# A decode kernel whose first transfer becomes sixteen runs of K's first chunk

## The chip, the cores and the metric

The kernel runs on one core of a Trainium2 chip. The metric is device time in microseconds (us), less is better. The time before is the median of three runs; one further execution was profiled.

## The reference

One decoding step: attention over a window of a cache, and beside it a small mixer with an MLP, both fed by the same normalized input. All tensors are bf16.

```python
xn = _layernorm(x, axis=-1)                                   # x: 4 x 1 x 576
return x + _A_ref(xn, A_k_cache, A_v_cache, A_wq, A_wo) + _B_ref(xn, B_w1, B_w2, B_w3, B_w4)

# A: 32 query heads, 16 key/value heads, Dh = 128, the last W = 2048 of 8192 positions
q = (x @ wq) per head;  k, v = the window of the caches
o = softmax(q k^T * Dh ** -0.5) v
A = o @ wo                                                    # wq: 576 x 4096, wo: 4096 x 576

# B: S = 1, so that the shifts leave the halves of h empty
h  = gelu(layernorm(x) @ w1);  x1 = x + shifted(h) @ w2       # w1, w2: 576 x 576
B  = x1 + gelu(layernorm(x1) @ w3) @ w4                       # w3: 576 x 4608, w4: 4608 x 576
```

## The kernel before

Nearly all of the data is read once: the K window and the V window (32 MB each), `wq`, `w3`, `w4` and `wo` of about 5 MB each, `w1` and `w2` of 0.65 MB each. All these transfers are issued on SyncE's queue (SP). Only the input `x` and the output go over ScalarE's queue.

Each engine has a program of its own. The list `prog[engine]` is sorted by a key that is written by hand, and the engine issues its list in that order. A transfer that has to wait for a buffer waits on SP, and all that stands behind it in SP's list waits with it. `add_dma(pairs, skey, waits, key)` (line 194) puts one transfer for each pair into the list; its issue is line 199. Each transfer adds 16 to the semaphore named by `skey` when it has landed. SP's order at the start is `w1` (key -50), `w2` (-49), `wq` (-48), `w3` (-47), then the chunks of K with keys 0, 1, 2 and so on. The first two chunks wait for nothing. Chunks 2 and 3 wait until the query is computed (`q`), since `wq` lies in their place. From chunk 4 on, each waits until TensorE has transposed the chunk four before it.

A chunk of K (`kv_src`) is one batch entry and four key/value heads: 128 runs of 64 positions, 16 KB each, 2 MB together. Its source is a view of 32 x 4 runs, and run (i, g) goes to partition 4 i + g of one of four slots of `kring` (`kslot`). There are 16 chunks, so a loop of four turns goes over the four slots. In the loop TensorE waits, ahead of a slot's first block, for the slot's semaphore:

```python
landed = e.snap(16 * it + 16)
...
if j % NBLK == 0:
    e.wait_ge(S["k", j // NBLK], landed)
```

For each chunk TensorE transposes eight blocks (line 485), VectorE and ScalarE copy them from PSUM (lines 469 and 468), and TensorE forms the scores (line 492). Ahead of the loop stands the small chain: two layernorms of `x` (lines 305 to 318), the mixer with `w1` (line 397) and `w2` (line 405), the query with `wq` (line 369), and the first half of the MLP with `w3` (line 430). The last entry of that program makes TensorE wait for a GpSimd constant. After the loop come the softmax (lines 498 to 535), eight chunks of V of 4 MB (line 553), and the products with `w4` and `wo` (line 392).

Of the kernel before, what the change touches and what calls it, by code (L numbers as in the profile page):

```python
# [37 lines left out]
def bass_parallel_sum__sliding_block_cached__mixer_s_mlp__decode_kernel(  # L38
# [31 lines left out]
    with ExitStack() as ctx:  # L70
        def sb(name, shape, dt):
            return ctx.enter_context(nc.sbuf_tensor(name, shape, dt))

        def sem(name):
            return ctx.enter_context(nc.semaphore(name))
# [5 lines left out]
        kslot = lambda s: kring[:, s * UE:(s + 1) * UE]  # L81
# [49 lines left out]
        perm_bf = sb("perm_bf", [128, 128], BF16)  # L131
# [39 lines left out]
        S = {}  # L171
# [16 lines left out]
        def add(engine, emit, waits=(), sig=None, key=0.0, inc=None):  # L188
            seqc[0] += 1
            prog[engine].append(Op(emit, waits, sig, key, seqc[0], inc))  # L190

        def add_dma(pairs, skey, waits=(), key=0.0, engine="sp"):
            if skey not in S:
                S[skey] = sem("s_" + "_".join(str(k) for k in (skey if isinstance(skey, tuple) else (skey,))))
            dma_count[skey] = dma_count.get(skey, 0) + 16 * len(pairs)

            def emit(e):
                for o_, i_ in pairs:
                    e.dma_start(o_, i_).then_inc(S[skey], 16)  # L199
            add(engine, emit, waits, None, key)  # L200
            return ("dma", skey, dma_count[skey])
# [48 lines left out]
        for gl in range(2):  # L250
            for x in range(2 * NVS):
# [3 lines left out]
                  waits=["pick11"], sig=f"pick2{gl}{x}", key=-84 + 0.1 * (8 * gl + x))  # L255


        def mask_of(t, tag, view):
            add("dve", lambda e: e.tensor_reduce(out=t[:], in_=view, axis=AX.X, op=ALU.add), waits=["ident_f"], sig=tag, key=-8)
        add("dve", lambda e: e.tensor_reduce(out=par[:], in_=ident_f[:].rearrange("p (m a) -> p a m", a=2), axis=AX.X, op=ALU.add),  # L260
            waits=["ident_f"], sig="par", key=-29.5)
# [13 lines left out]
        def kv_src(cache, c):  # L275
            b, gq = CH[c]
            return cache[b, NU * gq:NU * gq + NU, Sk - W:Sk, :].rearrange("g (i t) d -> i g (t d)", t=NT)
# [7 lines left out]
        t_done = lambda c: f"T{NBLK * c + NBLK - 1}"  # L285
        for c in range(NC):
            w = [t_done(c - N_CB)] if c >= N_CB else (["q"] if c >= 2 else [])
            add_dma([(kslot(c % N_CB), kv_src(A_k_cache, c))], ("k", c % N_CB), w, c)
        for c in range(NCV):
            w = [f"PV{2 * (c - NVS) + 1}"] if c >= NVS else [t_done(NC - N_CB + 2 * c - 3)] if c >= 2 else ["h2_1"]  # L290
# [93 lines left out]
        for k in range(2):  # L384
            for g in range(2):
# [3 lines left out]
                    waits=["qTp"] + (["qpad_zero"] if k + g == 0 else []), sig=f"qT{2 * k + g}", key=-10 + 0.1 * k)  # L389
# [18 lines left out]
        for h in range(2):  # L408
# [3 lines left out]
                waits=[f"hs{h}"], sig="x1" if h else "x1a", key=-27 + 0.1 * h)  # L412
# [3 lines left out]
            waits=["hT", "ln3_sd"], sig="gelu_h", key=-25.9)  # L416
# [38 lines left out]
        def pe_MO(t0, t1):  # L455
# [4 lines left out]
                        ins = acc_mm(e, h, h2T_sb[:, t, :], w4_t[:, t, HALF * h:HALF * (h + 1)])  # L460
                return ins
            return f
        add("pe", lambda e: e.wait_ge(S["pool"], resolve("perm_bf")[1]), waits=["qT3"], key=-1)


        def evac(n):
# [4 lines left out]
        for n in range(NB):  # L471
            c, k = n // NBLK, n % NBLK
            if k == 0:
                add("dve", lambda e, c=c: e.tensor_copy(out=Qs[:, c % N_CB, :], in_=Qpad_t[:, 128 * (4 * CH[c][0] + CH[c][1]):][:, 0:128]),
                    waits=[f"SC{c - 2}"] if c >= 1 else ["qT3"], key=n)
# [12 lines left out]
        def emit_SC(e, k):  # L488
# [11 lines left out]
            waits=["rmax"], sig="negb", key=KS + 0.05)  # L500
        for q in range(4):
            add("act", lambda e, q=q: e.activation(out=P_sb[:, q, :], in_=Sps[:, q, :], func=ACTF.Exp,
                                                   bias=negb[:, 0:1], scale=scale, accum_out=rs4[:, q:q + 1]),
                waits=["negb"], sig=f"exp{q}", key=KS + 0.1 + 0.01 * q)
# [16 lines left out]
        for qt in range(4):  # L521
            k0 = KS + 0.9 + 0.1 * qt
            add("pe2", pe_PT(qt), waits=[f"PTx{q}" for q in range(4)] + (["pick217"] + [f"E{NB - 1 - k}" for k in range(4)] if qt == 0 else []),
                sig=f"PTp{qt}", key=k0)
            if qt % 2 == 1:
                add("dve", lambda e, qt=qt: e.tensor_copy(out=PT_t[:, 512 * qt:512 * (qt + 1)], in_=ps[:, 4 + qt, :]),
                    waits=[f"PTp{qt}"], sig=f"PT{qt}", key=k0)
            else:
                add("act", lambda e, qt=qt: e.activation(out=PT_t[:, 512 * qt:512 * (qt + 1)], in_=ps[:, 4 + qt, :], func=ACTF.Copy),
                    waits=[f"PTp{qt}"], sig=f"PT{qt}", key=k0)  # L530
# [3 lines left out]
            waits=["rinv", "ident_f"], sig="diag", key=KS + 0.82)  # L534
        add("pe2", lambda e: e.matmul(rinvps, lhsT=ones_f[:], rhs=diag[:], start=True, stop=True),
            waits=["diag", "ones_f", "PT1"], sig="rinvp", key=KV + 0.5)
        add("dve", lambda e: e.tensor_copy(out=rinvB[:].rearrange("p (c u e) -> p c u e", u=NU, e=2),
                                           in_=rinvps.rearrange("p (u c e) -> p c u e", u=NU, e=2)),
            waits=["rinvp"], sig="rinvB", key=KV - 2)
# [29 lines left out]
        for bp in range(NPAIR):  # L569
            k0 = KV + 2 * NVS * (bp + 1) - 0.5  # L570
            add("dve", lambda e: e.tensor_scalar(out=tmp[:], in0=ps[:, 0, 128:256], scalar1=maskd[:, 1:2], scalar2=None, op0=ALU.mult),  # L571
                waits=[f"PV{2 * NVS * (bp + 1) - 1}", "maskd"], sig=f"F{bp}", key=k0)
# [4 lines left out]
                waits=["rinvB", f"fold{bp}"], sig=f"O{bp}", key=k0 + (3 if bp == 0 else 0.2))  # L577
# [5 lines left out]
            waits=["OR"], sig="ORT", key=KE + 0.3)  # L583
# [42 lines left out]
        def resolve(w):  # L626
            if isinstance(w, tuple):
                return S[w[1]], w[2]
            s_, val = ev_val[w]
            return S[s_], val  # L630
# [20 lines left out]
        e = nc.tensor  # L651
        emit_program("pe", "pe", e)
        with nc.Fori(0, N_LOOP, engines=[PE]) as it:
# [7 lines left out]
            for j in range(LB):  # L661
                emit_T(e, j, wait)
                if j % NBLK == 2:
                    k = (j // NBLK - 1) % N_CB
# [53 lines left out]
```

## Time and profile before

| what | value |
|---|---|
| median of three runs | 213.97 us (213.81 to 213.98) |
| the profiled execution, its own time | 213.93 us |
| its span, first to last instruction | 212.6 us |
| TensorE busy | 172.5 us, 81% of the span |
| VectorE, ScalarE, GpSimd busy | 111.9, 58.6, 15.6 us |
| DMA | 88.65 MB, mean 417 GB/s |

The profile's page gives, after the busy times of the engines, the span in 40 equal slices: a digit is the busy share of a slice in tenths, and the rows for DMA give the share of 16 DMA engines and the GB/s. A DMA row of a queue has packets, MB and the share of 16 engines' span that the packets took. In a table of windows each row has the stretch, the busy time and number of instructions of each engine, the TensorE clock, the share of the DMA engines and GB/s. Rows of a timeline begin with start and duration and may end with the idle time before and what ended it; "SPq" is SyncE issuing transfers. Lists of issues have the size of one transfer and the median time from issue to landing.

### The profile page before, as it was taken

Reading aid. Unit: us, or ns where it says so; the run is one execution under the profiler, and the core shown is the slowest. Engines: PE = TensorE matmul, PEld = TensorE weight load, DVE = VectorE, ACT = ScalarE, POOL = GpSimd, SP = SyncE. Lnnn points to the kernel's source line nnn. Section 1 sums busy time; section 2 is a strip of 40 time slices with the busy share of each in tenths; the row PEclk is TensorE's granted clock in tenths of the full one; section 3 lists DMA queues with packets and bytes.
Section 4 is the critical chain, followed back from the end, with each engine's and each line's share of the span. In section 5 each row is a group of like instructions: output and inputs, shape, how many; then the busy total and the mean of one; then the engine's idle time right before and its main releaser. Section 6 shows DMA issues by size and latency. Waiting matters only on the chain.

```text
span 212.6 us, 4856 instructions
## 1 busy us (share of the span) xinstructions
PE 172.5 (81%) x2212; PEld 133.7 (63%) x2216; DVE 111.9 (53%) x168; ACT 58.6 (28%) x69; POOL 15.6 (7%) x38
## 2 busy tenths in 40 slices
PE   1456147999999999999996089999989598997495
PEld 0222014888878888887774048988868487883262
DVE  5433200477776777777764869995575444003000
ACT  2004001366665566666656520000000000000000
POOL 8991000000000000000000000000000000000000
PEclk9997855899999999999999589999999889999799
DMA  6999999999999999999999999999999999999993
GB/s 242 453 444 445 429 396 416 432 425 427 429 416 438 432 422 429 435 422 424 432 444 438 444 407 459 413 425 453 407 444 438 419 425 410 451 476 393 407 408 131
DMA packets 5066, 88.65 MB, mean 417 GB/s; under 512 B 568, under 2 KB 704, under 8 KB 1216
## 3 DMA queue, kind: packets, MB, share of 16 engines
q1 hardware_dynamic: 5040, 88.49, 97.7%
q8 instruction: 8, 0.13, 0.3%
q14 instruction: 2, 0.02, 0.0%
q10 hardware_dynamic: 16, 0.01, 0.0%
HBM read 88.49 MB, written 0.00 MB: 416 GB/s over the span
## 4 chain that ended last, share of the span: by engine, by line
DMA 47%; PE 45%; DVE 4%; SPq 1%; ACT 1%; issue 1%
PE ps L485 23%; DMA vring<-in_A_wo_dram 15%; DMA vring<-in_B_w_dram 13%; DMA vring<-in_A_v_cache_dram 12%; PE ps L553 11%; DMA kring<-in_A_k_cache_dram 7%; PE ps L492 6%; PE ps L430 2%; SPq L199 1%; DVE vring L520 1%; DVE rmax L498 1%; DVE ktb L545 1%; PE ps L514 1%; PE ps L347 1%; ACT ktb L468 0%
## 5 line engine op out<-in xcount | busy, mean ns | idle before, releaser
L469 DVE COPY ktb<-ps 128x1024 bf16<-128x1024 bf16 x80 | 53.8, 689 | 23.5 <-PE ps L485 23.4
L485 PEld LDWEIGHTS ps<-perm_bf,kring 128*128 128x128 bf16 x1024 | 58.2, 98 | 8.3 <-issue 7.6
L485 PE MATMUL ps<-perm_bf,kring 128*128 128x128 bf16 x1024 | 61.7, 220 | 0.2
L468 ACT ACTIVATE ktb<-ps 128x1024 bf16<-128x1024 bf16 x48 | 48.0, 1023 | 32.5 <-PE ps L485 32.1
L545 DVE TENSOR_TENSOR ktb<-kring,mH_bf 128x4096 bf16<-128x4096 bf16 x16 | 36.2, 2286 | 14.6 <-PE ps L553 14.6
L553 PE MATMUL ps<-vring,ktb 128*128 128x256 bf16 x256 | 30.3, 282 | 4.3 <-DMA vring<-in_A_v_cache_dram 3.5
L553 PEld LDWEIGHTS ps<-vring,ktb 128*128 128x128 bf16 x256 | 25.7, 101 | 8.5 <-issue 3.6
L553 PE MATMUL ps<-kring,ktb 128*128 128x256 bf16 x256 | 28.6, 273 | 0.9 <-DMA kring<-in_A_v_cache_dram 0.9
L553 PEld LDWEIGHTS ps<-kring,ktb 128*128 128x128 bf16 x256 | 25.0, 98 | 4.5 <-issue 1.1
L608 ACT ACTIVATE out_sb<-ps 4x288 bf16<-4x288 f32 x1 | 0.4, 399 | 84.6 <-PE ps L392 84.6
L492 PE MATMUL ps<-ktb,Qs 128*32 128x512 bf16 x272 | 17.8, 382 | 1.2 <-ACT ktb L468 1.2
L430 PE MATMUL ps<-vring,xs 128*8 128x320 bf16 (+1 forms) x72 | 4.5, 429 | 7.6 <-DMA vring<-in_B_w_dram 7.6
L492 PEld LDWEIGHTS ps<-ktb,Qs 128*32 128x32 bf16 x272 | 5.7, 96 | 6.7 <-DVE ktb L469 1.4
L514 PE MATMUL ps<-vring,pick_bf 128*32 128x256 bf16 x64 | 3.9, 411 | 6.4 <-DVE rinv L532 6.4
L609 DVE CAST out_sb<-ps 4x288 bf16<-4x288 f32 x1 | 0.4, 449 | 15.7 <-PE ps L392 15.7
L392 PE MATMUL ps<-vring,h2T_sb 128*4 128x288 bf16 x72 | 6.2, 347 | 3.1 <-DMA vring<-in_B_w_dram 3.1
L571 DVE TENSOR_SCALAR tmp<-ps,maskd 128x128 f32<-128x128 f32 x2 | 0.7, 350 | 14.8 <-PE ps L553 14.8
L430 PEld LDWEIGHTS ps<-vring,xs 128*8 128x8 bf16 x72 | 2.1, 110 | 9.8 <-DMA vring<-in_B_w_dram 8.0
L330 PE MATMUL ps<-ident_bf,xp_bf 4*128 4x4 bf16 x15 | 0.8, 163 | 8.1 <-DVE xp_bf L314 5.0
L392 PEld LDWEIGHTS ps<-vring,h2T_sb 128*4 128x4 bf16 x72 | 3.7, 101 | 5.8 <-DMA vring<-in_B_w_dram 3.6
L514 PEld LDWEIGHTS ps<-vring,pick_bf 128*32 128x32 bf16 x64 | 2.0, 118 | 8.2 <-DVE rinv L532 6.9
L239 POOL MEMSET ktb<- 128x8192 bf16 x1 | 6.9, 6924 | 0.0
(93 smaller groups left out, 78.6 us busy)
## 6 DMA issues: line engine op xcount, KB each, us to landing
kring<-in_A_k_cache_dram SPq DMA_DIRECT2D x16, 2048.0 KB, 13.8
vring<-in_A_v_cache_dram SPq DMA_DIRECT2D x4, 4096.0 KB, 24.6
kring<-in_A_v_cache_dram SPq DMA_DIRECT2D x3, 4096.0 KB, 34.0
vring<-in_B_w_dram SPq DMA_DIRECT2D x2, 5184.0 KB, 25.1
kring<-in_A_wq_dram SPq DMA_DIRECT2D x1, 4608.0 KB, 15.7
kring<-in_A_v_cache_dram SPq DMA_DIRECT2D x2, 2048.0 KB, 27.4
vring<-in_A_wo_dram SPq DMA_DIRECT2D x1, 1872.0 KB, 26.9
vring<-in_A_wo_dram SPq DMA_DIRECT2D x1, 1440.0 KB, 29.8
```

Of the source, the lines that this page charges most:

```text
L199: e.dma_start(o_, i_).then_inc(S[skey], 16)
L239: P(lambda e: e.memset(ktb[:, NKT // 2 * 1024:NKT * 1024], 0.0), key=-92, inc=(("E", LB - 2), 1))
L347: ins = e.matmul(ps[:, w, :], lhsT=zeros_bf[:, 0:128], rhs=zeros_bf[:, :], start=True, stop=True)
L392: return e.matmul(ACC[h], lhsT=lhsT, rhs=rhs, start=start, stop=stop, tile_position=(0, 32 * h), skip_group_check=True)
L430: ins = e.matmul(H2ps[k][32 * j:32 * j + 2 * B].rearrange("b (p t) -> b p t", t=n), lhsT=x_at(2, s_), rhs=w[:, :, 9 * j + t0:9 * j + t0 + ...
L468: return "act", lambda e: e.activation(out=ktbuf[:, n % NKT], in_=tb[n % 4], func=ACTF.Copy)
L469: return "dve", lambda e: e.tensor_copy(out=ktbuf[:, n % NKT], in_=tb[n % 4])
L485: ins = e.transpose(tb[j % 4][:, t, :], kslot_t(k)[:, 8 * kb + t, :], perm_bf[:])
L492: ins = e.matmul(Sps[32 * u:32 * u + 32, q, :].rearrange("p (t i) -> p t i", t=16), lhsT=Qs[:, k, 32 * u:32 * u + 32], rhs=ktgrp[:, (4 * k ...
L514: ins = e.matmul(ps[32 * j:32 * j + 32, 4 + qt, 256 * ih:256 * (ih + 1)].rearrange("p (t a e) -> p t a e", a=NPAIR, e=2), lhsT=pick_bf[:, ...
L545: return lambda e: e.tensor_tensor(out=PTpad[:, n % 4], in0=PTv[:, qt, NH * h:NH * (h + 1), bp, :].unsqueeze(2).to_broadcast([128, NH, NX, ...
L553: ins = e.matmul(ps[:, 0, 0:256], lhsT=PTpad[:, 2 * (k % 2) + h, 2 * g:2 * g + 2].rearrange("p t h e -> p (t h e)"), rhs=vslot(k)[:, Dh * ...
```

## The change

Chunk 0 of K comes in four transfers in place of one. The first, 16 runs for partitions 0, 8, 16, ..., 120 (256 KB), is issued with key -60, ahead of all other transfers on SP, on the slot's old semaphore. The other three keep the chunk's place in the order (key 0): 16 runs for partitions 4, 12, ..., 124, 32 runs for partitions 2, 6, ..., 126, and 64 runs for the odd partitions. They count on a semaphore of their own, `k0`, to 48. TensorE waits for it once, in the entry that stands last before the loop; the loop's wait for 16 on the slot's semaphore is met, in the first turn, by the first transfer alone.

```diff
         for c in range(NC):
             w = [t_done(c - N_CB)] if c >= N_CB else (["q"] if c >= 2 else [])
+            if c == 0:
+                k0, s0 = kslot(0), kv_src(A_k_cache, 0)
+                add_dma([(k0[0:128:8], s0[0:32:2, 0:1])], ("k", 0), (), -60)
+                ev_k0 = add_dma([(k0[4:128:8], s0[1:32:2, 0:1]), (k0[2:128:4], s0[:, 2:3]), (k0[1:128:2], s0[:, 1:4:2])], "k0", (), 0)
+                continue
             add_dma([(kslot(c % N_CB), kv_src(A_k_cache, c))], ("k", c % N_CB), w, c)
...
-        add("pe", lambda e: e.wait_ge(S["pool"], resolve("perm_bf")[1]), waits=["qT3"], key=-1)
+        add("pe", lambda e: e.wait_ge(S["pool"], resolve("perm_bf")[1]), waits=["qT3", ev_k0], key=-1)
```

## The prediction

> **What bounds the kernel now.** I read the page from the top: the span, the forty slices, the queues, then the chain.
>
> ```profile
> span 212.6 us, 4856 instructions
> DMA  6999999999999999999999999999999999999993
> GB/s 242 453 444 445 429 396 416 432 425 427 429 416 438 432 422 429 435 422 424 432 444 438 444 407 459 413 425 453 407 444 438 419 425 410 451 476 393 407 408 131
> q1 hardware_dynamic: 5040, 88.49, 97.7%
> DMA 47%; PE 45%; DVE 4%; SPq 1%; ACT 1%; issue 1%
> ```
>
> The chain's shares would let one think that the matmuls bound half of the time. The slices say otherwise: the transfers are at 9 in all but the first and the last slice, and SP's queue q1 alone keeps the sixteen DMA engines (lanes, below) busy for 97.7% of the span. The windows of busy time give the rates:
>
> ```profile
> 0.00:1.80 1.80, 0.42 (x1) 0.10 (x1) 0.00 (x0) 0.40 (x1) 1.14 (x8) 1.00 0.01 3
> 1.80:2.40 0.60, 0.18 (x1) 0.00 (x0) 0.16 (x1) 0.60 (x1) 0.60 (x2) 1.00 0.92 199
> 2.40:5.00 2.60, 0.00 (x0) 0.00 (x0) 2.23 (x7) 0.49 (x2) 2.45 (x7) 1.00 1.01 401
> 5.00:30.00 25.00, 10.31 (x92) 4.99 (x96) 8.05 (x28) 2.68 (x5) 11.46 (x24) 0.84 1.01 431
> 30.00:95.00 65.00, 63.65 (x1062) 51.41 (x1056) 41.64 (x74) 35.97 (x38) 0.00 (x0) 0.93 1.01 427
> 95.00:208.00 113.00, 95.83 (x1045) 76.28 (x1047) 59.35 (x60) 18.08 (x24) 0.00 (x0) 0.94 1.00 430
> 210.00:212.60 2.60, 0.66 (x8) 0.26 (x8) 0.45 (x1) 0.40 (x1) 0.00 (x0) 1.00 0.01 2
> ```
>
> The last column is GB/s, the one before it the share of the lanes in use. From 5 to 208 us the rate stays at 427 to 431, whatever the rows are: 16 lanes at 430 / 16 = 26.9 GB/s each. So the time is: 1.80 us until the first byte, 0.5 us lost to the ramp, 88.49 MB / 0.430 = 205.8 us of stream, and a short tail (208.1 of 212.6). A lane that loses time has no spare rate to win it back with. What an edit does to the stream moves the end one for one; what it does to an engine must first use up that engine's slack.
>
> **The change, part by part.** The first rows here are SP's queue in the timeline; the last two are from the list of transfers issued ahead of 2.8 us, with KB each and the time from issue to landing.
>
> ```profile
> 0.80 0.85 SPq L199 DMA_DIRECT2D ktb<-in_B_w_dram  x2
> 1.70 0.42 SPq L199 DMA_DIRECT2D kring<-in_A_wq_dram  x1
> 2.17 0.52 SPq L199 DMA_DIRECT2D vring<-in_B_w_dram  x1
> 2.73 1.25 SPq L199 DMA_DIRECT2D kring<-in_A_k_cache_dram  x2
> kring<-in_A_k_cache_dram SPq DMA_DIRECT2D x1, 2048.0 KB, 33.0
> ktb<-in_B_w_dram SPq DMA_DIRECT2D x2, 648.0 KB, 4.3
> ```
>
> *Bytes.* None are added: a chunk of 2048 KB is 128 runs of 16 KB, and 16 + 16 + 32 + 64 = 128. A run of 16 KB takes one lane 16.384 / 26.9 = 0.609 us; a chunk in its old form is eight such runs per lane, 4.87 us.
>
> *Issues.* SP issues six transfers in a row before it first waits for TensorE; now it is nine. Three more at about 0.6 us (1.25 / 2) are 1.9 us of SP. One stands ahead of w1 and delays w1's issue by about 0.4; the others stand where the queue already holds w1, w2, wq and w3: K's first chunk lands 33.0 us after its issue at 2.73, so what is issued 2 us later still waits in line. Cost nothing; without that cover, 1.9 us. Completion marks of the three extra transfers: nothing that these rows can show.
>
> *The start.* This is what can be won. In 1.80:2.40 the rate was 199 of 430, a loss of 0.60 x (1 - 199/430) = 0.32 us; in 2.40:5.00 it was 401, a loss of 2.60 x (1 - 401/430) = 0.18 us. The first 1.80 us, between barrier, issue and first byte, any first transfer must pay too. With 16 runs each lane gets one run at once and has 0.6 us of work, during which w1's 128 short rows (648 KB / 128 = 5 KB) are handed out. The 0.18 belongs to w1's and w2's rows, which stay as they are. So the gain lies between 0 and 0.5 us. Part of the 0.32 is a slow first access, which a 16 KB run has as well; I take 0.1, near the lower end.
>
> *The spread.* Here is the unknown cost. Every transfer of q1 in this trace fills 128 partitions; none shows what 16, 32 or 64 runs with gaps between their partitions do. If lanes have ways of their own into the memory's partitions whatever the rows, it costs 0. If the gapped forms bring two lanes onto one way at a time, each run takes 2 x 0.609, and the eight runs per lane of this chunk lose 8 x 0.609 = 4.87 us, 0.61 of it in the first transfer. That holds if the lanes go in step; lanes a whole run apart would not meet. Transfers of 28 to 40 us, in slices of 0.3 us, show which:
>
> ```profile
> GB/s 0 0 492 273 546 328 546 273 601 273 601 273 601 218 655 218 601 273 601 273 546 328 492 328 492 382 492 382 492 382 437 437 437 437 437 437 437 382 437 437
> ```
>
> Packets start in a beat: high and low slices alternate with K's run of two slices (0.6 us), three to one at the strongest. The lanes are neither in full step nor evenly spread when this chunk comes by. So I take half of 4.87, 2.4 us, of which the first transfer, where all start together, has 0.6. Both ends stay in the range.
>
> [...]
>
> *Who waits for what has come later.* Rows of the timeline, then two of the chain in order of time:
>
> ```profile
> 2.24 0.45 DVE L305 BATCH_NORM_STATS2 stats<-x_sb 4x6 f32<-4x288 bf16 x1 [2.24 <-DMA x_sb<-in_A_x_dram]
> 8.46 2.32 PE L397 MATMUL ps<-ktb,xs 128*8 128x288 bf16 x9 [0.78 <-DVE xs L336]
> 20.51 23.07 SPq L199 DMA_DIRECT2D kring<-in_A_k_cache_dram  x3
> 29.68 4.49 PE L430 MATMUL ps<-vring,xs 128*8 128x320 bf16 x72 [7.56 <-DMA vring<-in_B_w_dram]
> 37.54 2.16 PE L485 MATMUL ps<-perm_bf,kring 128*128 128x128 bf16 x24
> 45.36 3.71 PE ps L485 x64
> 49.06 0.98 PE ps L492 x16
> 94.51 14.58 DMA kring<-in_A_k_cache_dram
> ```
>
> w1 landed about 4.3 us after its issue, near 5.1 to 5.5, and its first matmul (L397) waited for VectorE until 8.46: 3 us of cover for the 0.6 to 1.2. x comes over ACT's queue and may now meet a 16 KB run: at worst 1.2 us on the layernorm, which runs into the 7.56 us that L430 waits for w3. The release of the third chunk's transfer (20.51) may come 1 us later, with the queue filled until two chunks past 29.6. w3 itself is 0.6 to 1.2 later, and so K's first transposes (37.54). The new wait for the rest of chunk 0 stands on TensorE ahead of the loop; behind it are all transposes and scores. The chunk landed at 2.73 + 33.0 = 35.7, 1.8 us ahead of L485, so only a loss beyond that shows there. Even then TensorE works off a chunk in 3.71 + 0.98 = 4.69 us, and the stream delivers one in 2.097 MB / 0.427 = 4.91; TensorE catches up and is waiting for chunk 15 (14.58 us from its issue) as before. All this costs nothing beyond the stream's own loss.
>
> *Sum.* -0.1 (start) + 2.4 (spread) = +2.3 us. The profiled execution took 213.93 us, its span 212.6 and 1.33 around it; the median shown is 213.97, 0.04 more. 213.93 + 2.3 = 216.2, in the median 216.3.
>
> **The rivals.** *The start is won and the spread is free* (chance 0.25). For it: all lanes ran alike on rows of 5, 16 and 41 KB, so a lane's own limit would explain 26.9 GB/s, and 0.5 us of ramp is there to be had. Then the ramp's 0.32 and part of the 0.18 go: about 213.97 - 0.45 = 213.5. It decides if gapped runs keep 0.61 us each.
>
> *Nothing to be seen* (0.15). The spread is free, and the first access is as slow as before: a gain of 0.1, 213.9. This is also what is left if the small first transfer starts as late as w1 did: the bytes are only in another order.
>
> *Only the starting group pays* (0.15). In the first transfer all lanes go in step and lose 0.6; by 30 us they are far enough apart. +0.6 - 0.1, with up to 0.6 for the second group of 16: 214.5 to 215.1.
>
> *The forecast* (0.45): loss in all four parts, +1.5 to +4.8, 215.5 to 218.8, likeliest 216.3.
>
> That the transfer isn't first can be set aside: its key of -60 sorts ahead of w1's -50, and it waits for nothing.
>
> **How the numbers follow.** Two of these end slower by over 0.2%, 0.60; one is within, 0.15; one is faster, 0.25. 0.2% is 0.43 us, about what a measurement of this kernel can tell from no change. Range: from the faster case, 213.5, to 218.4, near the upper bound 213.97 + 4.87 - 0.1 = 218.7; what is left out is about 2 in 10, at the two far ends. Within the forecast alone: 215.5 to 218.4.
>
> **What would show it.** In the changed profile the window 1.80:2.40 should show more GB/s than 199 if the start is won. A first group at half rate would show about 215 GB/s from about 2 to 3 us. In place of chunk 0 (about 30 to 35 us) the rate should fall below 427, the later windows should be at 427 to 430 as now, and L430 should start 0.5 to 1.2 later than 29.68. If chunk 0 passes at 427 or more, the forecast's step on the spread is wrong, and the time is 213.5 to 213.9. If the loss appears beyond 95 us, my claim on the covers is wrong.

## The result, and the profile after

The changed kernel takes 215.24 us in the median (215.09 to 215.62, six runs), the kernel before 213.98 (213.81 to 214.20, six runs). The ratio is 1.0063, 95% interval 1.0053 to 1.0074: slower by 1.26 us. The profiled execution took 215.53 us, its span is 214.2.

The page after, first the span, the forty slices and SP's queue, then the chain by engine:

```profile
span 214.2 us, 4860 instructions
...
DMA  5999899999999999999999999999999999999993
GB/s 176 452 441 482 372 367 419 431 428 424 410 431 438 428 413 435 438 428 412 435 468 428 422 428 428 438 435 419 441 422 435 441 407 428 442 477 403 388 414 132
...
q1 hardware_dynamic: 5088, 88.49, 97.5%
...
DMA 63%; PE 28%; DVE 4%; SPq 2%; ACT 1%; issue 1%
```

The bytes are the same, and the queue is as full as before (97.5% against 97.7%); the first slice fell from 242 to 176 GB/s, and slices five and six are low at 372 and 367, where before they had 429 and 396. In the windows of busy time (last column GB/s) the loss has two places, the start and the stretch that begins at 30 us; from 95 us on nothing differs:

```profile
1.80:2.40 0.60, 0.18 (x1) 0.00 (x0) 0.05 (x1) 0.60 (x1) 0.60 (x2) 1.00 0.84 220
2.40:5.00 2.60, 0.00 (x0) 0.00 (x0) 2.23 (x6) 0.48 (x2) 2.46 (x7) 1.00 0.84 258
5.00:30.00 25.00, 10.08 (x84) 4.67 (x84) 8.27 (x29) 2.69 (x5) 11.49 (x25) 0.84 1.01 434
30.00:95.00 65.00, 62.00 (x1036) 49.23 (x1038) 40.40 (x71) 35.35 (x37) 0.00 (x0) 0.96 1.00 421
95.00:208.00 113.00, 95.02 (x1057) 76.46 (x1057) 60.83 (x63) 19.43 (x25) 0.00 (x0) 0.95 1.00 430
```

A packet's bytes are counted where it starts, so a window shorter than a packet misleads: 220 GB/s in 1.80:2.40 is not a better start, it is eight runs of 16 KB that had only begun, and the first of them ends at 3.18 us. Finer slices show the start. These are the transfers from 0 to 4 us in slices of 0.1 us, before:

```profile
GB/s 0 0 0 0 0 0 0 0 0 0 0 0 0 0 0 0 0 46 311 259 156 52 156 259 259 467 363 415 415 415 363 415 415 363 311 467 363 467 363 519
```

and after:

```profile
GB/s 0 0 0 0 0 0 0 0 0 0 0 0 0 0 0 0 0 35 0 12 0 328 655 328 328 328 164 164 0 328 0 104 208 156 52 156 415 207 259 207
```

The 46 and the 35 at 1.7 us are the input x on ACT's queue. w1 came in the next slice, at 1.8 us; the 16 runs come at 2.1 to 2.2. And where before the rate was near full from 2.5 us, after it stays low to the end of this row, above 363 in one slice of the last ten. The chain before has w1's issue (start, us, what):

```profile
0.80 0.37 SPq L199
```

SP's timeline after has the issues:

```profile
0.80 0.61 SPq L199 DMA_DIRECT2D kring<-in_A_k_cache_dram  x1
1.47 1.03 SPq L199 DMA_DIRECT2D ktb<-in_B_w_dram  x2
2.54 0.43 SPq L199 DMA_DIRECT2D kring<-in_A_wq_dram  x1
```

The first issue takes 0.61 us, where w1's took 0.37 and w1's and w2's together 0.85. Further along, TensorE's timeline after:

```profile
31.46 4.40 PE L435 MATMUL ps<-vring,xs 128*8 128x320 bf16 x72 [7.79 <-DMA vring<-in_B_w_dram]
...
37.77 0.81 PE L352 MATMUL ps<-zeros_bf 128*128 128x512 bf16 x3 [0.64 <-DMA kring<-in_A_k_cache_dram]
...
38.42 1.50 PE L490 MATMUL ps<-perm_bf,kring 128*128 128x128 bf16 x24
```

The MLP (old line 430) begins 1.8 us later, the first transposes (old line 485) 0.9 later, and TensorE waits 0.64 us for the rest of chunk 0.

The views count packets in slices; the traces also hold the start, size and duration of each packet, and some figures below are taken from these records.

### The profile page after: what moved, and what is told of

Its sections match the earlier page's. It is cut to its first block, busy times and chain, and to the rows that moved or that the text cites. A ratio compares the mean times of both kernels' runs of the same rounds, so it can differ in the third digit from the quotient of the medians.

```text
span 214.2 us, 4860 instructions
## 1 busy us (share of the span) xinstructions
PE 170.5 (80%) x2212; PEld 131.9 (62%) x2216; DVE 112.2 (52%) x168; ACT 59.3 (28%) x69; POOL 15.7 (7%) x38
## 3 DMA queue, kind: packets, MB, share of 16 engines
q1 hardware_dynamic: 5088, 88.49, 97.5%
## 4 chain that ended last, share of the span: by engine, by line
DMA 63%; PE 28%; DVE 4%; SPq 2%; ACT 1%; issue 1%
DMA kring<-in_A_k_cache_dram 36%; DMA vring<-in_A_wo_dram 16%; PE ps L490 12%; DMA vring<-in_A_v_cache_dram 12%; PE ps L558 10%; PE ps L497 4%; SPq L199 2%; DVE vring L525 1%; DVE rmax L503 1%; DVE ktb L550 1%; PE ps L519 1%; ACT ktb L473 0%; PE ps L352 0%; ACT Qpad L507 0%; PE ps L397 0%
## 5 line engine op out<-in xcount | busy, mean ns | idle before, releaser
L490 PEld LDWEIGHTS ps<-perm_bf,kring 128*128 128x128 bf16 x1024 | 57.4, 98 | 9.6 <-issue 7.4
L473 ACT ACTIVATE ktb<-ps 128x1024 bf16<-128x1024 bf16 x48 | 48.7, 1023 | 31.8 <-PE ps L490 31.0
L558 PE MATMUL ps<-kring,ktb 128*128 128x256 bf16 x256 | 30.2, 281 | 2.6 <-DMA kring<-in_A_v_cache_dram 2.6
L558 PE MATMUL ps<-vring,ktb 128*128 128x256 bf16 x256 | 28.6, 273 | 4.1 <-DMA vring<-in_A_v_cache_dram 2.2
L558 PEld LDWEIGHTS ps<-kring,ktb 128*128 128x128 bf16 x256 | 25.7, 101 | 6.9 <-issue 2.8
L558 PEld LDWEIGHTS ps<-vring,ktb 128*128 128x128 bf16 x256 | 24.8, 98 | 7.4 <-issue 3.3
L435 PE MATMUL ps<-vring,xs 128*8 128x320 bf16 (+1 forms) x72 | 4.4, 421 | 7.8 <-DMA vring<-in_B_w_dram 7.8
L435 PEld LDWEIGHTS ps<-vring,xs 128*8 128x8 bf16 x72 | 2.1, 111 | 10.0 <-DMA vring<-in_B_w_dram 8.1
L397 PE MATMUL ps<-vring,ORT 128*4 128x288 bf16 x64 | 4.6, 286 | 2.3 <-DMA vring<-in_A_wo_dram 2.3
```

What stands on the lines that cost most here:

```text
L397: return e.matmul(ACC[h], lhsT=lhsT, rhs=rhs, start=start, stop=stop, tile_position=(0, 32 * h), skip_group_check=True)
L435: ins = e.matmul(H2ps[k][32 * j:32 * j + 2 * B].rearrange("b (p t) -> b p t", t=n), lhsT=x_at(2, s_), rhs=w[:, :, 9 * j + t0:9 * j + t0 + ...
L473: return "act", lambda e: e.activation(out=ktbuf[:, n % NKT], in_=tb[n % 4], func=ACTF.Copy)
L490: ins = e.transpose(tb[j % 4][:, t, :], kslot_t(k)[:, 8 * kb + t, :], perm_bf[:])
L558: ins = e.matmul(ps[:, 0, 0:256], lhsT=PTpad[:, 2 * (k % 2) + h, 2 * g:2 * g + 2].rearrange("p t h e -> p (t h e)"), rhs=vslot(k)[:, Dh * ...
```

## The experiments

Differences are medians against the kernel before in the same batch, whose median lay between 213.97 and 214.10 us.

**Chunk 0 in four parts, all at its place**

```diff
-add_dma([(k0[0:128:8], s0[0:32:2, 0:1])], ("k", 0), (), -60)
+add_dma([(k0[0:128:8], s0[0:32:2, 0:1])], ("k", 0), (), -0.5)
```

> All four parts of chunk 0 stand at the chunk's old place; w1 is again the first transfer, and no byte is added. Theory A (two lanes of a 16-run transfer with step 8 write through one way into the memory): both groups of 16 lose about one run of 0.61 us each where they stand, the groups of 32 and 64 nothing; the start is that of the kernel before (199 GB/s in 1.80:2.40); 214.6 to 215.2 us, and below 430 GB/s only near 30 to 33 us. Theory B (the loss is the late start alone: a first byte 0.39 us later, and no more): within 0.1 us of the kernel before. Theory C (all three gapped forms lose): 216 us or more.

215.45 us, +1.42, ratio 1.0066 (1.0052 to 1.0079). Theory B is out. The time lies 0.25 us above the range that I gave for theory A and 0.55 below that for C, so this run alone does not rule C out; the next one does. Splitting alone, with no early transfer, costs as much as the whole change.

**32 runs first, no group of 16**

```diff
-add_dma([(k0[0:128:8], s0[0:32:2, 0:1])], ("k", 0), (), -60)
-ev_k0 = add_dma([(k0[4:128:8], s0[1:32:2, 0:1]), (k0[2:128:4], s0[:, 2:3]), (k0[1:128:2], s0[:, 1:4:2])], "k0", (), 0)
+add_dma([(k0[0:128:4], s0[:, 0:1])], ("k", 0), (), -60)
+ev_k0 = add_dma([(k0[2:128:4], s0[:, 2:3]), (k0[1:128:2], s0[:, 1:4:2])], "k0", (), 0)
```

> The first transfer is 32 runs, partitions 0, 4, 8, ...; the rest of chunk 0 comes at its place as 32 and 64 runs, so there is no transfer of 16 runs. Theory A: no run takes much over 0.61 us once it is under way, nothing is lost at 30 to 33 us, and only a start later than w1's is left: 213.9 to 214.4 us. If a first transfer with few long runs is bad in itself, or the step of 4 as bad as that of 8: 214.8 us or more. If the idea of the change pays once the spread is right: 213.5 to 213.8 us.

214.35 us, +0.32, ratio 1.0015 (1.0006 to 1.0024): theory A again. The window 30 to 40 us of four kernels, in the order before, after, four parts in place, 32 first, each in a fence of its own:

```profile
30.00:40.00 10.00, 8.71 (x125) 5.43 (x122) 1.37 (x4) 1.53 (x3) 0.00 (x0) 0.55 1.01 429
```
```profile
30.00:40.00 10.00, 7.42 (x121) 4.68 (x126) 1.14 (x4) 1.31 (x3) 0.00 (x0) 0.73 1.02 398
```
```profile
30.00:40.00 10.00, 8.67 (x134) 4.81 (x134) 1.79 (x4) 1.84 (x3) 0.00 (x0) 0.71 0.97 382
```
```profile
30.00:40.00 10.00, 7.69 (x122) 4.64 (x126) 1.10 (x3) 1.26 (x3) 0.00 (x0) 0.71 0.99 419
```

One group of 16 lowers the rate by 31 GB/s, two by 47; without one it is 10 lower, which is within the packets that start just ahead of or behind the window's edge. The groups of 32 and 64 are nearly free: +0.32 us in all, the late start included.

The packets' durations show the loss itself. A packet of 16 KB takes 0.61 us in the median. Of those that begin between 27 and 45 us (the list takes in the three kernels of the next experiment), these were longer:

| kernel | packets over 0.70 us | longest, us | time of all beyond 0.612 each, us per lane |
|---|---|---|---|
| before | 2 | 1.11 | 0.04 |
| after | 34 | 1.16 | 0.87 |
| four parts in place | 52 | 1.26 | 1.43 |
| 32 first | 2 | 1.12 | 0.06 |
| 16 extra, by eight | 48 | 1.44 | 1.05 |
| 16 extra, by four | 5 | 1.11 | 0.07 |
| 16 extra, adjacent | 48 | 2.22 | 2.16 |

The last column is within 0.2 us of what each kernel lost at this place. A group by eight has packets of up to 1.16 us in the change and 1.44 as an extra, about twice the usual time, the adjacent one up to 3.6 times (2.22), and packets of the transfers beside the group are long too: 34 in the change and 48 with either extra are over 0.70 us, where the one group has 16.

**16 extra runs behind chunk 0: by eight, by four, adjacent**

Three kernels read 256 KB of chunk 0 once more into an unused place of `vring`; they differ in the partitions alone.

```diff
+s0 = kv_src(A_k_cache, 0)
+ev_d = add_dma([(vring[P, 3 * UE:4 * UE], s0[0:32:2, 0:1])], "dup", (), 0.5)   # P = 0:128:8, 32:96:4, 0:16
```

> The kernel before with 16 runs of 16 KB (256 KB) read once more, behind chunk 0, to an unused place of vring at partitions 0, 8, ..., 120. Bytes alone: +0.61 us (214.6). Theory A, two lanes to a way: +1.2 us (215.2), a little less if lanes are apart. Rival D (a transfer with one run per lane is slow whatever its partitions, or the source's step of 32 KB is): the same as the kernel with partitions 32 to 92, whatever that is.

> The same extra 16 runs from the same source, to partitions 32, 36, ..., 92. [...] Theory A: +0.61 us, its bytes alone (214.6), 0.6 less than step 8. Rival D: no difference to step 8.

> The extra 16 runs behind chunk 0, now to partitions 0 to 15. [...] The extra by step 8 cost 1.8 us (0.6 of it bytes), by step 4 from 32 0.7. With a cost that goes with the number of lanes on a way: +3 to +4.5 us, 217 to 218.5. If only the kind of step mattered, a dense group would cost no more than step 4: 214.7.

By eight: 215.84 us, +1.81, ratio 1.0090 (1.0077 to 1.0104). By four from 32: 214.75, +0.72, ratio 1.0034 (1.0021 to 1.0048). Adjacent: 216.70, +2.60, ratio 1.0123 (1.0108 to 1.0139). The bytes are 0.61 in each. What the partitions add is 1.2, 0.1 and 2.0 us. Rival D is out: same source, same number of runs, and nearly no loss where the partitions are 32 to 92. Theory A undershot the first (I expected 0.6 beyond the bytes) and overshot the third (I expected +3 to +4.5 in all). How many lanes would meet on one way at partitions 0 to 15, on which that range rests, no run shows. Transfers from 28 to 40 us in slices of 0.3 us, by eight:

```profile
GB/s 0 0 328 437 382 492 328 546 328 546 273 601 273 601 273 601 273 601 218 601 164 328 273 164 109 382 328 164 546 273 601 218 655 218 546 328 546 328 492 382
```

by four:

```profile
GB/s 0 0 328 382 382 492 328 546 218 655 218 655 218 655 218 655 218 655 164 710 164 656 219 655 164 655 218 655 164 710 164 710 164 710 164 710 164 656 164 710
```

adjacent:

```profile
GB/s 0 0 273 492 328 546 328 546 328 492 382 492 273 601 218 655 164 710 164 656 164 109 219 164 164 55 109 55 218 437 164 218 437 218 601 273 601 273 601 273
```

Each pair of slices is one run per lane. By four the beat passes the 16 runs (from about 34 us) unbroken. By eight it breaks for eight or nine slices, 2.4 to 2.7 us, although the group itself is two slices of work: the runs of chunk 1 behind it are held up too, which fits a price of more than a doubling. Adjacent it breaks for twelve or so.

Why the three groups differ no run shows; their order and their prices beyond the bytes are measured.

**The first half of the change by itself**

The same extra transfer by eight, with key -60 in the place of 0.5.

> The first half of the change by itself: 16 runs of chunk 0, step 8, are issued first, as an extra copy to an unused place of vring; chunk 0 comes whole at its place, so nothing can be lost there. By the sum of the earlier runs: 0.61 us of bytes, 0.3 us for a start 0.36 us later, 0.3 us for two lanes on one way: +1.2 us, 215.2 to 215.4, and 427 GB/s at 30 to 40 us. If the start costs no more than 32 runs first did: +0.9, 214.9. If the change's loss is all at the chunk's place: +0.6, 214.6.

215.01 us, +1.04, ratio 1.0051 (1.0037 to 1.0065). Less its bytes that is 0.43 us for the start, between the first two of the three times that I had named. At 30 to 40 us the rate is 421 GB/s, and between 27 and 45 us only two packets are over 0.70 us, as before. The interval is 0.3 us wide to each side, so 0.43 can't be told from the lateness of the 32 first (0.3). The packets give no sign that the step of eight costs anything at the start: the sixteen first runs took 0.91 us in the median here and 1.02 after the change, both by eight, but 1.08 with 32 first, by four, and 0.98 with the whole chunk first. All first runs are longer than 0.61, whatever their partitions.

**Why the first byte is late: chunk 0 whole, w1 in parts, wq in part, w1 by columns, w1 by halves**

All put another form of transfer first. The edits, in this order:

```diff
+add_dma([(kslot(0), kv_src(A_k_cache, 0))], ("k", 0), (), -60)            # whole chunk first
+[(w1_t[0:128:4], r1[0:128:4]), (w1_t[2:128:4], r1[2:128:4]), (w1_t[1:128:2], r1[1:128:2])]
+add_dma([(wq_t[0:128:4], rq[0:128:4])], "wq", (), -60)                    # the rest of wq as 32 and 64
+[(w1_t[:, 0:1296], r1[:, 0:1296]), (w1_t[:, 1296:2592], r1[:, 1296:2592])]
+[(w1_t[0:64], r1[0:64]), (w1_t[64:128], r1[64:128])]
```

> Chunk 0 whole, in its old form of 128 runs, is the first transfer (key -60). If the source makes the issue long, SP takes 0.55 to 0.62 us for it and the first packet is at 2.1 to 2.2 us, with nothing lost later: +0.2 to +0.4 us, as for 32 runs first. If few runs were the cause, the first packet is at 1.80 and the time is that of the kernel before. w1 lands 4.9 us later; the chain to L430 keeps 2 us of its 7.56.

> Chunk 0 as in the kernel before; w1 comes in three parts of 32, 32 and 64 runs in the place of one (steps 4, 4 and 2, none of 16 runs). It asks where the late first byte comes from. If a cached-K source takes SP longer to issue (0.56 to 0.61 us against 0.37) and that is all, the first packet is at 1.80 us as before. If few runs make it late, it is at 2.1 to 2.2. Few runs with no late start would show what the idea can win: the rate in 1.80:2.40 over 199 GB/s. Each part of 32 is 0.39 us of stream and an issue takes 0.42, so no gain beyond 0.1 us is expected: 213.9 to 214.2 us.

> The idea of the change with the spread and the source mended: the first transfer is 32 runs of wq (36 KB each, partitions 0, 4, 8, ...; 1.18 MB, 2.7 us of stream), then w1, w2, and the rest of wq as 32 and 64 runs. If wq is issued as fast as w1 (0.42 us), the first byte is at 1.80 to 1.85; nothing is lost to shared ways; gain up to the ramp of 0.3 us: 213.7 to 214.0 us. w1 lands 2.7 us later, near 8 us, against its first use at 8.46. If it is no better than the kernel before, the ramp is not caused by the many short runs but by the first access.

> w1, still first, in two transfers of 128 runs: the first and the second half of each run (2.6 KB, the source stepping over the other half). All 128 partitions, many runs, the same source tensor. Every first transfer so far whose runs do not adjoin in the source had its first packet at 2.15 to 2.22 us; w1 whole, whose runs adjoin, at 1.80. If gaps between the runs in the source are the cause: SP issues it in 0.55 to 0.6 us and the first packet is at 2.15 or later, +0.3 us or more. If the number of runs is the cause: 1.80 and 0.37.

> w1, still first, as partitions 0 to 63 and then 64 to 127: fewer runs, but each group adjoins in the source. If gaps in the source are the cause of the late start: issue 0.37 us, first packet at 1.80. If any form but a full one of 128 partitions starts late: 2.15. [...]

| first transfer | first issue, us | packets begin in the slice at, us | time against before, us |
|---|---|---|---|
| w1, 128 runs (the kernel before) | 0.37 | 1.8 | |
| w1 by columns, 128 runs | 0.37 | 1.8 | +1.17 |
| 16 runs of chunk 0 (after) | 0.61 | 2.1 | +1.26 |
| 32 runs of chunk 0 | 0.56 | 2.1 | +0.32 |
| w1 in parts, 32 runs | 0.56 | 2.1 | +1.28 |
| wq, 32 runs | 0.56 | 2.1 | +0.30 |
| w1 by halves, 64 runs | 0.57 | 2.1 | +1.92 |
| chunk 0 whole, 32 x 4 runs | 0.63 | 2.2 | +2.02 |

Three times lie above what I had expected: w1 in parts (215.38 us against 213.9 to 214.2), wq in part (214.40 against 213.7 to 214.0) and w1 by halves (215.97 against at most 215.0). The start is late in every form but a plain one over 128 partitions. My first reason, the cached-K source, fell with w1 in parts, whose source is w1's. My second, gaps between the runs in the source, fell with the last two: by columns the source has gaps and the start is on time, by halves it has none and the start is late. The issues of w1 and w2 in these two, min, median and max in ns, by columns:

```profile
L199 SPq DMA_DIRECT2D ktb<-in_B_w_dram x3: 374/416/662, 0.8 to 1.7; - x3
```

and by halves:

```profile
L199 SPq DMA_DIRECT2D ktb<-in_B_w_dram x3: 568/572/578, 0.8 to 2.1; - x3
```

Transfers from 0 to 4 us, by columns:

```profile
GB/s 0 0 0 0 0 0 0 0 0 0 0 0 0 0 0 0 0 23 141 130 156 52 63 104 233 389 363 389 415 389 415 389 389 415 415 415 415 415 493 441
```

and by halves:

```profile
GB/s 0 0 0 0 0 0 0 0 0 0 0 0 0 0 0 0 0 35 0 12 0 363 104 259 259 259 207 311 156 259 467 156 363 259 156 311 104 259 207 363
```

Why SP takes longer over the other forms no run shows. Three of the times have further parts, which no run separates. In parts of 32, w1 brings 0.39 us of stream with each issue of 0.56 or more, and in 2.40:5.00 the rate is 265 GB/s where it was 401: lanes would stand still between the parts. By halves the rate there is 251. My upper bound held 0.77 us, half of the 1.54 that w1's 648 KB are at 430 GB/s, for lanes that hold each other up; that they do so there no run shows, and where the 1.92 comes from is open. By columns the ten runs lie far apart (214.19 to 215.72). The profiled one, 0.6 us slower, has 335 GB/s in 2.40:5.00, so there the loss is at the start; why isn't settled.

The whole chunk first cost 2.0 us, where I expected 0.2 to 0.4. A cover seems to be used up. Its timeline:

```profile
34.86 4.19 PE L430 MATMUL ps<-vring,xs 128*8 128x320 bf16 x72 [6.81 <-DMA vring<-in_B_w_dram]
...
41.60 1.50 PE L485 MATMUL ps<-perm_bf,kring 128*128 128x128 bf16 x24
```

and two of its windows:

```profile
48.00:50.00 2.00, 2.00 (x40) 1.47 (x33) 1.16 (x2) 0.60 (x2) 0.00 (x0) 1.00 0.89 352
50.00:52.00 2.00, 2.00 (x39) 1.99 (x37) 1.80 (x5) 1.68 (x2) 0.00 (x0) 1.00 0.95 360
```

The MLP waits for w3 until 34.86 in place of 29.68, the first transposes start at 41.60 in place of 37.54, and with them everything that waits for a slot of K. At 48 to 52 us the rate falls to 352 and 360, where the kernel before has 438 and 426. These windows are only three packets long, and their lanes' share of 0.89 and 0.95 does not mean idle lanes: by the packets' records the lanes stand idle for 0.19 us between 40 and 60 us (0.09 before), while packets beyond their usual time cost 1.10 us per lane (0.13 before); some of 16 KB take 0.8 to 2.2 us. So the loss comes with the late transposes, but that it comes from a queue that runs low, and why the packets are long, isn't shown. I had looked at what waits for w1 and not at what waits for w3.

**wq whole and first**

```diff
-ev_wq = add_dma([(wq_t, runs(A_wq))], "wq", (), -48)
+ev_wq = add_dma([(wq_t, runs(A_wq))], "wq", (), -60)
```

> Nothing is split; wq, whose 128 long runs (36 KB) adjoin in the source, is issued ahead of w1 and w2. It is the idea of the change (long runs first, so that lanes have work while short ones are handed out) in a form with no gap and no shared way. First packet at 1.80 and less lost than 0.5 us up to 5 us: 213.7 to 214.0 us. w1 lands 11 us later, near 16 us; its chain then ends close to w3's landing at 29.6, and if it ends later, chunk 0 starts later and the time rises above 214.2.

214.13 us, +0.08, ratio 1.0006 (0.9997 to 1.0015): no difference. This first transfer has long runs, no gap and all 128 partitions. Its issue takes 0.37 us (min, median and max in ns):

```profile
L199 SPq DMA_DIRECT2D kring<-in_A_wq_dram x1: 374/374/374, 0.8 to 0.8; - x1
```

and the transfers from 0 to 4 us are:

```profile
GB/s 0 0 0 0 0 0 0 0 0 0 0 0 0 0 0 0 0 46 1475 737 369 369 369 1106 369 737 0 0 369 0 0 0 0 0 0 0 0 0 737 0
```

Packets begin at 1.8 us and each lane has work for over a microsecond; still nothing is won (I had expected 213.7 to 214.0 us). The packets' records say where the time goes: the sixteen first runs of 36 KB take 2.03 us in the median, all of that size 1.36. Before the change w1's sixteen first rows take 0.39, all of that size 0.20. So the ramp is no want of work: the first runs are slow themselves, short or long, and a first transfer of long runs is not spared. Why they are slow no run shows. No version tried beats the kernel before.

## Why the prediction was right, and where not

**The bound held.** The stream at 427 to 430 GB/s sets the end. In every profile the last packet of SP's queue ends later than before by as much as the execution is longer, within 0.2 us. TensorE's later start didn't reach the end: with 32 first the transposes began 0.9 us later too, and the time was +0.32.

**The spread was the right step, and its term was too large.** I took 2.4 us, half of 4.87, for all four parts. The runs give 0.83 at the chunk's place (1.26 less the 0.43 of the start; the packets there say 0.87), 0.7 for each group of 16 with all parts in place, and at the start, where I put 0.6, nothing that can be told from the lateness. The step that failed is that the groups of 32 and 64 would lose as the 16 do: with 32 first they passed at +0.32 in all, the size of the late start. A loss of 0.61 us in each of the two groups of 16 and none in the others, 1.2 in all, would have been nearer, though it has half of its loss in the first transfer, where none shows. That two lanes meet on one way, from which the 4.87 was worked out, no run shows; what the runs show is packets of up to 1.16 us where the change's second group of 16 passes. Of the cases I named, the measured 215.24 fits none: it stands between "only the starting group pays" with its second group (up to 215.1) and the lower end of the forecast (215.5). That it lies in the range is in part luck: a spread sized more than a microsecond too large and a start taken as a gain of 0.1 where it lost 0.43 erred in opposite ways. My allowance for lanes out of step was wrong in kind: a group of 16 costs more than its own doubling (0.83 at the place, 1.2 as an extra, against 0.61), since packets beside it are long as well. Why the extra one costs more than the one in the change, and which lane takes which partitions in a group of 32 or 64, no run shows.

**The start had the wrong sign.** I wrote that any first transfer must pay the first 1.80 us, and took the gain between 0 and 0.5. The issue of 16 runs takes 0.61 us, w1's issue comes 0.67 later and not 0.4, the packets begin at 2.1 to 2.2, and the start costs 0.43 instead of winning 0.1. The row that could have warned stood in the trace: K's chunks take longer to issue (1.25 for two) than w1 and w2 (0.85 for two). The ramp's 0.32 us was not to be won either: wq first brought no gain. The slow first access, which I had named and given only a part of the ramp, falls on long runs more than on short ones (0.66 us more for a run of 36 KB, 0.19 for a row of 5 KB).

**The covers held for this change.** x, w1 and the release of chunk 2 cost nothing that shows: x comes 0.1 us later (2.35), w1's matmuls still wait for VectorE (8.67), and the query's matmuls, which now wait 1.23 us for wq, release chunk 2 later with the rate from 5 to 30 us at 434 GB/s. The new wait did show, 0.64 us ahead of the zeroing matmuls, and was caught up as forecast. The matmuls on w3 (L430, now L435) came 1.8 us later; I had said 0.5 to 1.2. One trace says little here: with all parts in place, where nothing ahead of w3 differs from before, they came 0.75 later (30.43).

**A sign that I named was no test.** More than 199 GB/s in 1.80:2.40 was to show a start won. It rose to 220 while the start was lost.

## What to carry to other kernels

In a kernel bound by its transfers, as here, a lane's lost time comes back nowhere: in the profiles the last packet ended 1.62 us later, and the execution took 1.60 us more. Before splitting a transfer, measure what the partitions of each part cost: here sixteen runs to 32 to 92 in steps of four cost 0.1 us beyond their bytes, to 0 to 120 in steps of eight 1.2. Measure an idea's best case by itself before paying for its machinery: wq first showed with one changed key that there was no ramp to win (+0.08 us). And read a window of rates only where it is longer than several packets, of 0.61 us each for 16 KB here.

## What the hardware showed that I had not expected

A first transfer over 128 partitions in plain form is issued in 0.37 us and its packets begin at 1.8; with 16, 32 or 64 runs, or as K's 32 x 4, it takes 0.56 to 0.63 and they begin at 2.1 to 2.2, whatever the source. The first runs of the stream take 0.91 to 1.08 us in the median where a run of 16 KB otherwise takes 0.61. Sixteen extra runs of 16 KB to partitions 0, 8, ..., 120 cost 1.2 us beyond their bytes, the time of two whole runs, and runs beside them are long as well; to partitions 0 to 15 they cost 2.0 us, and to 32, 36, ..., 92 only 0.1.
